# Attention and a state-space scan on one core: weight pieces by DMA, first projections split, one more rotation on VectorE, and a new hand-written order

## The chip, the cores and the metric

The kernel runs on one core of a Trainium2 chip. Its engines take their instructions in order, each from its own queue: TensorE (PE, with weight loads shown apart as PEld), VectorE (DVE), ScalarE (ACT), GpSimd (POOL) and SyncE (SP), which here only issues DMAs. The metric is the device time of one execution in microseconds (us). Before the change it is 131.46 us, the median of three runs (131.37 to 131.47).

## The reference

Two independent parts work on 2048 tokens of width 448, and their results stand side by side in the output (2048 x 896, bfloat16).

```python
# A: attention, 16 heads of 28, each token looks at 8 tokens: itself and 2, 4 ... 14 before it
qkv = x @ wqkv
logits = einsum("bhsd,bhswd->bhsw", q, kg) * 28 ** -0.5     # masked where the index is negative
o = einsum("bhsw,bhswd->bhsd", softmax(logits), vg)
a = o @ wo
# B: a diagonal complex recurrence over time, 448 states
Lam_bar = exp(dt * Lam);  Bu = x @ B_bar.T
h = Lam_bar * h + Bu[t]                                     # for each of 2048 tokens
y = 2 * real(hseq @ Cmat.T) + x * Dskip
out = concatenate([a, y], axis=-1)
```

## The kernel before

Every piece of work is a small function with a short name (marked `@op`), and the string `ORDER` lists some 550 steps. The steps are carried out in that order, so each engine's queue is the string with the other engines' steps left out. In a step such as `QK021@65` the digits behind the name are arguments and those behind `@` the PSUM banks (eight of 2 KB in a partition) that it takes; a dot or an equals sign at the end of a copy out of PSUM says ScalarE or VectorE. A bank is free again only when the step that reads it is done.

**Part A.** x is cut into two halves `u` of 1024 tokens, and each into two blocks `s` of 512. Half 0 is transposed on TensorE (`XI`, `XA`, `XH`, copied into `xT` by `xi`, `xa`, `xh`), half 1 by four DMA transposes (L164), which SP issues behind the loads of half 1 (`xA1`, L148) and of the first part of B's x (`x_load(0)`, L158). The projections contract over 448 = 3 x 128 + 64 rows. `QK(u, m, k)` does group `m` of q or k (0 to 6, even for q and odd for k; 6 holds the last columns of both) for both blocks: with `k` = 0 the three full matmuls of each block, with `k` = 1 the two matmuls over the last 64 rows. Of those, block 0 uses rows 0 to 63 of weights and x, and block 1 rows 64 to 127. So the last 64 weight rows stand twice in `wq[:, 3]`: by DMA in rows 0 to 63 (L135) and copied to rows 64 to 127 by GpSimd (L214, L215). `QS(m, s)` is one block's projection at once, three full matmuls (L347) and the one of 64 rows (L348), for the first two groups of half 0. `wq6` is a tight copy of the last columns, made by GpSimd (L216, L218). `qk` and `qh` copy the results out of PSUM. `V_`/`v` do the same for the values.

`P` multiplies q with four shifted views of k on VectorE (L378; 28 products, of 2048 elements in each partition). `E_` adds them up over the head's 28 channels on TensorE (L390, L394), and `lt`, `TR`, `tr`, `sma`, `smb`, `smc` scale, transpose and normalize. `AL`/`al` line the weights up, `ad` and `sp` send them through DRAM into a banded matrix `PT`, `AV`/`av` multiply it with the values, `W_`/`w`/`ow` multiply with `wo` and store.

**Part B.** The 2048 tokens become 512 groups of T = 4. B's matrix comes transposed by `BD` (one DMA, L651), x by four DMAs `xt` (L675). `BU(g, jp, k)` projects x for state group `g` (7 of them), with k as in `QK`, `BR` adds the rotated previous position, `z` and `y` copy out of PSUM; `UP`, `sa`, `sb`, `sd` scan over the group sums on VectorE, `DN`/`dn` finish them. Then the state before a group is rotated into the group's positions j = 0, 1, 2 for each g, 21 rotations, in one of two ways:

- `H_(j, g)` is one 128 x 512 matmul (L767), and `h(j, g)` adds its result to Z on VectorE (L772);
- `sw(g)` sends a half-swapped copy to `BT` by two DMAs (L790, L791), and `ha`/`hb` (or `ka`/`kb`, the same code) do two VectorE steps (L796, L800).

The order before has twelve of the first kind and nine of the second. At the end 16 blocks `C(j, ct)` are each seven matmuls of 448 columns (L831), `c` adds the skip term on VectorE (L837) and `oc` stores 112 KB from SP (L841). `xd` prepares the skip term. `tf`, `ts`, `rb`, `ca`, `cs` and the `p` steps make tables and coefficients; `tx` and `tz` touch an activation function so that ScalarE loads its table then.

Of the kernel before, what the change touches and what calls it, by code (L numbers as in the profile page):

```python
# [37 lines left out]
qh000. qh011. v000= qh101. QK110@70 P010 E_00@4 qh001. E_02 E_04 xt3 ts13 QK111 P031 QK121@31 qh100. QK141@65 qh111.
QK140 hc0 qk111. ts23 qk141. ts25 QK120 qk140. qk120. QK100@05 qk121. P050 qk110. V_410@63 hc1 qh110. QK101 P061 P011
qk100. qk101. V_411 E_01@1 tf2 ts02 P051 LC P030 E_03 tf6 E_05 QK130@72 P060 E_06 QK151@05 v411. v410. QK131 qk130.  # L40
P101 qk131. P111 lt00 P110 QK150 qk151. V_500@36 V_501 qk150. V_511@72 lt01 P131 v501. V_401@45 TR0@0 V_400 ts06 V_510
E_11@1 tr0. P100 v500. v401. v400. v511. v510. P130 E_13 E_10@6 sma0 smb0 P121 P141 BU401@03 OZ P150 BU201@54 BU301@27
BU300 P120 XR P151 z30. ci1. ci2. BU200 z20. CD1 BR31 ts12 ci3. BU400 z40. P140 z31. ci0. BU000@25 BR21 E_12 z21. E_14
E_15 P160 BU001 BU311@07 z00. CD3 P161 E_16 lt11 lt10 BR41 z41. BU310 BR32 TR1@4 tr1. z32. BU210@21 CD0 smc0 CD2 AL0@6
BR01 BU101@34 sma1 al0. z01. BR33 rb3 BU100 z10= ca6 BU010@06 smb1 xd1 ad0 ts16 BR11 BU211 tx z11. BU111@53 cs6 BU011
BR02 OP smc1 z33. BR22 BU110 z02. BR03 ca3 z03. BR12 BU500@40 UP0 pm3 z12. BR13 z22. BR23 y0. UP3 cs3 AL1@5 z13. z23.
wo UP1 y1. pm0 xd2 AL2@2 pm4 sp0 UP2 y3. BU410@63 y2. al1= BU411 al2. BU501 ts22 BU511@75 z50. BU601@12 BR42 ca4 BU600
ad1 z60. BR51 z51. BU510 sa0 sb0 sd0 DN1@4 BU611@10 cs4 BR52 z42. BR43 AL3@6 ad2 dn1 z52. al3. BR61 z43. sa2 BR53
H_01@4 pm1 sp1 DN0@7 dn0 z53. BU610 z61. BR62 UP5 ts26 UP4 AV001@6 av001. y5. AV020@7 y4. av020. pm2 h01 z62. AV021@2
sb2 ad3 av021. AV031@4 av031. sd2 AV010@6 AV011@5 AV000@3 sp2 AV030@7 av011. DN3@1 W_11@2 H_11@4 av000. av030. av010.  # L50
w11. W_31@5 sa4 sb4 sd4 h11 DN2@3 dn2 ca0 W_00@7 W_10@6 w10. w00. W_01@2 sp3 dn3 DN5@4 w31. dn5 cs0 W_21@6 BR63 H_02@3
ow31 DN4@7 dn4 H_22@1 H_20@5 h22 h20 w01. z63. H_12@4 h12 ow10 ow11 H_10@2 W_30@7 UP6 H_13@1 ha24 W_20@5 h10 ca1 y6.
ca5 AV111@0 av111. AV121@4 AV130@2 ow01 ow00 w30. sa6 av130. AV131@0 AV100@7 h02 av100. sw4 hb24 AV120@2 AV110@3
av131. av110. AV101@7 H_21@0 av120. w20. ow20 sb6 ha14 ow30 av121. w21. W_60@3 ow21 W_70@2 cs1 av101. H_23@5 sd6 sw5
DN6@4 W_50@6 W_40@7 ca2 ha15 dn6 sw6 h13 h23 cs2 W_41@4 w41. hb14 ow41 W_51@1 cs5 C33@5 w50. ha25 w60. ow60 w40. ha16
H_00@4 hb25 W_61@6 ka05 hb15 hb16 W_71@3 C31@7 ow50 w70. w71. ha26 H_03@2 h00 c31 C12@3 h21 C30@4 hb26 xd0 C20@7 ka04
w51. kb05 ow70 C10@1 c10 C32@0 w61. c20 oc31 C13@6 c12 oc12 xd3 c13 c32 ow71 oc13 oc10 ka06 C21@1 C23@7 c30 c21 oc30
C22@3 oc21 c23 oc20 kb04 oc23 oc32 ow51 h03 kb06 c33 C11@6 c22 c11 oc11 C00@0 c00 oc00 C03@4 ow61 oc33 c03 oc03 C01@1
c01 C02@7 oc22 ow40 c02 oc01 oc02
"""  # L60

@with_exitstack
def kernel(
# [276 lines left out]

    @op
    def QS(m, s):

        p = ps()
        pp.setdefault(("qk", 0, m), {})[s] = p
        for kt in range(3):
            PE.matmul(p[:], wqk(m, slice(0, 128), kt), xT[:, 0, 4 * s + kt], start=(kt == 0), stop=False)  # L347
        PE.matmul(p[:], wqk(m, slice(64 * s, 64 * s + 64), 3), xT[64 * s:64 * s + 64, 0, 3], start=False, stop=True)  # L348
# [571 lines left out]
```

## Time and profile before

| what | value |
|---|---|
| median of three runs | 131.46 us |
| the profiled execution, its own time | 131.66 us |
| its span, first to last record | 129.95 us |
| first matmul of a projection (QS00) starts | 6.52 us |
| VectorE's first copy of the second x block (xa10) starts | 9.31 us |
| last 640-byte weight loads land (second L135) | 10.57 us |
| last DMA transpose of half 1 of x lands | 22.27 us |
| first matmul that uses half 1 (QK161) | 23.85 us |
| first scan step (sa0) starts | 71.79 us |
| last matmul ends, last add ends | 126.48, 127.14 us |

The profile's busy time of an engine is the time with at least one instruction running. Matmuls are pipelined, so the time that one costs is the distance from its start to the next one's start. Idle time stands in brackets, with what ended it. A DMA is issued (the time on SP's queue) and lands later, when its data is in place; "landing" is the latter.

### The profile page before, as it was taken

The numbers are of one execution on the slowest core, as the hardware profiler recorded it, in microseconds if no ns is written. First come the engines' busy times: TensorE is split into PE (matmuls) and PEld (weight loads), VectorE is DVE, ScalarE is ACT, GpSimd is POOL, SyncE is SP. The second block draws the span as 40 slices with busy tenths as digits, with TensorE's granted clock in tenths as the row PEclk, the third lists the DMA queues.
The fourth block names the chain that finished last, engine by engine and source line by source line (L and its number), as shares of the span: only waits on it lengthen the run. The fifth ranks groups of instructions, "written<-read, shape, count | busy, mean of one in ns | idle before, by whom it ended". The sixth has DMA issues, their size and how long they took to land.

```text
span 129.9 us, 2872 instructions
## 1 busy us (share of the span) xinstructions
PE 123.9 (95%) x1071; PEld 62.8 (48%) x1071; DVE 119.0 (92%) x211; ACT 90.9 (70%) x185; POOL 23.0 (18%) x45
## 2 busy tenths in 40 slices
PE   6899999999989999999999999999999999999990
PEld 6843445343423434435446335945694554555540
DVE  5679999999999999999999999999999999999941
ACT  3459899999974999987999987999889651000000
...
GB/s 99 196 315 270 308 214 166 229 221 237 167 204 213 226 192 343 240 136 71 203 186 138 273 259 239 209 153 91 184 29 89 110 129 6 34 71 139 144 208 110
DMA packets 44838, 22.91 MB, mean 176 GB/s; under 512 B 31064, under 2 KB 43800, under 8 KB 44824
## 3 DMA queue, kind: packets, MB, share of 16 engines
...
q8 instruction: 8, 0.13, 0.4%
...
HBM read 11.56 MB, written 6.29 MB: 137 GB/s over the span
## 4 chain that ended last, share of the span: by engine, by line
PE 57%; DVE 28%; ACT 9%; issue 3%; DVEq 0%
PE ps L238 21%; DVE pr L378 13%; PE ps L831 13%; PE ps L524 4%; PE ps L701 4%; PE ps L511 3%; DVE Ak L796 3%; PE ps L256 2%; PE ps L347 2%; DVE Z L800 2%; DVE Z L772 2%; ACT kh L114 2%; ACT qf L114 1%; DVE Cw L667 1%; ACT qh_t L114 1%
## 5 line engine op out<-in xcount | busy, mean ns | idle before, releaser
L378 DVE TENSOR_TENSOR pr<-qf,kf 128x2048 bf16<-128x2048 bf16 x24 | 28.4, 1231 | 0.0
L238 PE MATMUL ps<-xbuf,BT 128*128 128x512 bf16 (+1 forms) x112 | 24.0, 379 | 0.0
L831 PE MATMUL ps<-Cw,Z 128*128 128x448 bf16 x112 | 21.8, 352 | 0.1
L238 PE MATMUL ps<-xT,wq 128*128 128x512 bf16 (+1 forms) x96 | 19.7, 380 | 0.0
L114 ACT CAST Z<-ps 128x512 bf16<-128x512 f32 (+1 forms) x34 | 15.7, 503 | 0.9 <-PE ps L713 0.5
L831 PEld LDWEIGHTS <-Z 128*128 128x128 bf16 x112 | 11.0, 98 | 10.5 <-issue 0.3
L238 PEld LDWEIGHTS <-BT 128*128 128x128 bf16 (+1 forms) x112 | 9.1, 97 | 11.7 <-issue 2.4
L524 PE MATMUL ps<-wo,oT 128*128 128x448 bf16 x64 | 13.6, 353 | 0.0
L238 PEld LDWEIGHTS <-wq 128*128 128x128 bf16 (+1 forms) x96 | 7.5, 97 | 11.5 <-issue 4.0
L238 PE MATMUL ps<-wq,xT 128*128 128x448 bf16 (+1 forms) x64 | 12.0, 353 | 0.0
L877 POOL MEMSET PT<- 128x4320 f32 x3 | 11.0, 3699 | 0.0
L837 DVE TENSOR_TENSOR xbuf<-ps,xnB 128x448 bf16<-128x448 f32 x16 | 9.2, 619 | 2.0 <-PE ps L831 1.7
L114 ACT CAST oT<-ps 128x512 bf16<-128x512 f32 x17 | 9.5, 626 | 1.4 <-PE ps L511 1.4
L114 ACT CAST ya<-ps 128x448 bf16<-128x448 f32 (+1 forms) x17 | 8.4, 557 | 2.8 <-issue 1.6
L663 ACT ACTIVATE ctmp<-Cw,c2t 64x448 f32<-64x448 bf16 x14 | 9.3, 666 | 0.3
L114 ACT CAST kf<-ps 128x512 bf16<-128x512 f32 x12 | 6.8, 596 | 3.5 <-PE ps L238 2.5
L524 PEld LDWEIGHTS <-oT 128*128 128x128 bf16 x64 | 6.1, 98 | 5.7 <-ACT oT L114 0.6
L511 PE MATMUL ps<-PT,v_s 128*32 128x135 bf16 (+1 forms) x256 | 8.4, 299 | 0.0
L238 PEld LDWEIGHTS <-xT 128*128 128x128 bf16 (+1 forms) x64 | 5.3, 97 | 5.5 <-issue 1.1
L772 DVE TENSOR_TENSOR Z<-ps,Z 128x512 bf16<-128x512 f32 x12 | 7.9, 682 | 0.0
L114 ACT CAST v_s<-ps 128x448 bf16<-128x448 f32 x15 | 7.3, 541 | 0.5 <-PE ps L238 0.5
L511 PEld LDWEIGHTS <-v_s 128*32 128x32 bf16 x256 | 7.1, 112 | 0.2 <-issue 0.2
...
## 6 DMA issues: line engine op xcount, KB each, us to landing
...
```

What stands on the lines that cost most here:

```text
L114: (ACT.copy if e == "A" else V.tensor_copy)(o, i)
L238: PE.matmul(o, l, r, start=(first and i == 0), stop=(not first and i == len(pairs) - 1 and not more[s]))
L378: V.tensor_tensor(t[:], q.unsqueeze(1).to_broadcast((128, 4, 512)), k4, ALU.mult)
L511: PE.matmul(p[32 * hh:32 * hh + 32, 128 * bl:128 * bl + n], v_s[:, t, 4 * hg + hh, :], PT[:, t % NS, (4 * hg + hh) // HS, (4 * hg + hh) % ...
L524: PE.matmul(p[:, 0:D], late["oT"][:, b // 4, hg, par, 128 * (b % 4):128 * (b % 4) + 128], late["wo"][:, hg, :], start=(hg == 0), stop=(hg ...
L663: ACT.activation(t[a:a + 64, 0:D], Cw[b:b + 64, g, :], ACTF.Copy, scale=c2t[a:a + 64, g:g + 1])
L701: PE.matmul(pp["z", g, j][:], rot(g, 0), late["Z"][:, g, j - 1, :], start=False, stop=True)
L772: V.tensor_tensor(zz, pp.pop(("h", j, g))[:], zz, ALU.add)
L796: e.scalar_tensor_tensor(t.rearrange("p (a n) -> p a n", a=2), prev(g), co2[:, 0, j, g:g + 1], late["Z"][:, g, j, :].rearrange("p (a n) -> ...
L831: PE.matmul(p[:, 0:D], z, Cw[:, g, :], start=(g == 0), stop=(g == G - 1))
L837: V.tensor_tensor(yo, pp.pop(("c", j, ct))[:, 0:D], xnB[:, ct, j, :], ALU.add)
L877: POOL.memset(late["PT"][:, 4 * i:4 * i + 4].rearrange("p t g n -> p (t g n)").bitcast(F32), 0.0)
```

## The change

- `QS` becomes `QA`: only the three full matmuls. The 64-row matmuls of groups 0 and 1 are now steps `QK001` and `QK011`, which add to the open sum in the banks that `QA` took.
- Rows 64 to 127 of `wq[:, 3]` and all of `wq6` come by DMA; GpSimd's five copies go. The first short piece (rows 0 to 63, 128 columns of q and k) is issued from ScalarE's queue, ahead of its three small loads `raw`.
- `H_23`/`h23` become `sw3`, `ha23`, `hb23`, so ten of the 21 rotations are on VectorE.
- The last block of C is (0, 3), in two column halves `CH1`, `CH0`, with their own adds and stores; block (0, 0)'s store and the last half's go out from ScalarE's queue.
- Copies out of PSUM change engine: to ScalarE xi00, xi21, xa11, qk001, v000, z10; to VectorE xi30, xi20, xh1, y0, y1, z50, z51.
- `ORDER` is written anew throughout. Among what moves: `XA10`, `XA11` and `XH1` come right behind the first `QA`; `rb2`, `rb3`, `rb1`, `pg` come ahead of the first product `P000`; `BD` comes ahead of all `xt` on SP; the first use of half 1 is `QK100` instead of `QK161`.

```diff
 ORDER = """
-WU@0 XI0@12 xi30. xi00= XI1@3 xi31. xi01= xi20. xi21= PP@4 pcopy pa pb pe pc QS00@5 pd_ QS10@6 qk010. XA10@7 XH1@1
-qk000. xh1. xt1 XA11@0 pf xt2 xa10= xa11= QS11@3 qk011. QK050@24 QK051 tf0 ts00 P000 QK021@65 QK041@70 QK031@13 tf1
...
+WU@0 XI0@12 xi30= PP@3 pcopy XI1@4 xi00. xi20= pa pb xi01= pe xi21. QA00@5 XA10@6 pd_ xa10= tf0 XA11@7 XH1@1 pc QA10@3
+BD xh1= xa11. tf3 QA01@2 QA11@0 xi31. QK011 QK031@67 QK001 pf pg pk rb2 qk000. QK021@41 qk010. ts00 QK030 qk030. QK020
+ts03 ts13 rb3 qk001. qk031. xt2 V_100@53 V_101 QK041@62 qk020. xt0 v100. qk011. v101. V_111@74 V_110 v110. QK040
+QK050@50 V_011@37 ts10 ts20 v111. rb1 qk040. V_001@46 P000 QK051 V_010 P020 V_000 qk041. ts23 qk050. QK100@25 P021 tf1
...
+oc21 ow70 oc12 oc01 c11 oc30 c00 oc11 oa00 c02 ch1 oc02 oh1 CH0@1 ch0 oh0
 """
...
+    def half_load(q, r, c, n):
+        q.dma_start(qk_s[r:r + 64, 3, :, c:c + n], qk_d[384:448, :, c:c + n])
+
+    half_load(ACT, 0, 0, 128)
     raw = const.tile([G, 3, 2, 64], BF16, tag="raw")
...
     def qk_load(c, n):
         for a in range(2):
             SP.dma_start(qk_s[:, 0:3, a, c:c + n], qk_d[0:384, a, c:c + n].rearrange("(f p) n -> p f n", p=128))
-        SP.dma_start(qk_s[0:64, 3, :, c:c + n], qk_d[384:448, :, c:c + n])
...
-    qk_load(128, 320)
+    qk_load(128, 256)
+    half_load(SP, 0, 128, 256)
+    half_load(SP, 64, 0, 384)
...
+    wq6 = s2.tile([128, 4, 2, 64], BF16, tag="wq6")
+    for a in range(2):
+        SP.dma_start(wq6[:, 0:3, a], qk_d[0:384, a, 384:D].rearrange("(f p) n -> p f n", p=128))
+    for s in range(2):
+        SP.dma_start(wq6[64 * s:64 * s + 64, 3], qk_d[384:448, :, 384:D])
...
-    wq6 = s2.tile([128, 4, 2, 64], BF16, tag="wq6")
-    POOL.tensor_copy(qk_s[64:128, 3, :, 0:128], qk_s[0:64, 3, :, 0:128])
-    POOL.tensor_copy(qk_s[64:128, 3, :, 128:384], qk_s[0:64, 3, :, 128:384])
-    POOL.tensor_copy(wq6[:, 0:3], qk_s[:, 0:3, :, 384:D])
-    for s in range(2):
-        POOL.tensor_copy(wq6[64 * s:64 * s + 64, 3], qk_s[0:64, 3, :, 384:D])
...
     def QK(u, m, k):
-        p = two("qk", u, m)
+        p = pp["qk", u, m] if u == 0 and m < 2 else two("qk", u, m)
...
-    def QS(m, s):
+    def QA(m, s):
 
         p = ps()
         pp.setdefault(("qk", 0, m), {})[s] = p
+        begun.add(("qk", 0, m))
         for kt in range(3):
             PE.matmul(p[:], wqk(m, slice(0, 128), kt), xT[:, 0, 4 * s + kt], start=(kt == 0), stop=False)
-        PE.matmul(p[:], wqk(m, slice(64 * s, 64 * s + 64), 3), xT[64 * s:64 * s + 64, 0, 3], start=False, stop=True)
...
+    @op
+    def oa(j, ct):
+        ACT.dma_start(out_b[j, ct // 2, ct % 2, :, D:2 * D], pp.pop(("yo", j, ct)))
+
+    LAST, CUT = (0, 3), (0, 224, 448)
+
+    @op
+    def CH(i):
+        j, ct = LAST
+        p = pp["ch", i] = ps()
+        n = CUT[i + 1] - CUT[i]
+        for g in range(G):
...
+            PE.matmul(p[:, 0:n], z, Cw[:, g, CUT[i]:CUT[i + 1]], start=(g == 0), stop=(g == G - 1))
+
+    @op
+    def ch(i):
...
+        V.tensor_tensor(yo[:, sl], pp.pop(("ch", i))[:, 0:CUT[i + 1] - CUT[i]], xnB[:, ct, j, sl], ALU.add)
+
+    @op
+    def oh(i):
+        j, ct = LAST
+        (ACT if i == 0 else SP).dma_start(out_b[j, ct // 2, ct % 2, :, D + CUT[i]:D + CUT[i + 1]], pp.pop(("yo", "part", i))[:, CUT[i]:CUT[i + 1]])
```

More of the change, by code (lines that the diff above doesn't have):

```diff
@@ L32 @@
 ORDER = """
-WU@0 XI0@12 xi30. xi00= XI1@3 xi31. xi01= xi20. xi21= PP@4 pcopy pa pb pe pc QS00@5 pd_ QS10@6 qk010. XA10@7 XH1@1
-qk000. xh1. xt1 XA11@0 pf xt2 xa10= xa11= QS11@3 qk011. QK050@24 QK051 tf0 ts00 P000 QK021@65 QK041@70 QK031@13 tf1
-qk051. ts10 ts01 ts20 QK030 QK020 qk031. qk020. pg qk050. qk030. tf4 BD pk QK040 QS01@4 V_001@36 qk041. V_111@21
-qk040. V_011@07 V_010 ts11 ts21 V_110 ts04 v010. v011. rb2 qk021. tz rb0 v110. V_000 P020 V_100@07 ts14 ts24 tf3 V_101
-P021 v001. rb1 v111. P040 QK161@52 QK061@61 v101. tf5 v100. P001 QK060 QK160 ts03 ts05 ts15 qh010. xt0 P041 qk001=
@@ L38 @@
[L38 to L57, printed above, removed]
@@ new lines @@
+QK050@50 V_011@37 ts10 ts20 v111. rb1 qk040. V_001@46 P000 QK051 V_010 P020 V_000 qk041. ts23 qk050. QK100@25 P021 tf1
+qk021. tf5 ts01 rb0 ts11 ts21 ts05 ts15 v011. P001 v010. QK101 qk100. P040 qk101. QK061@17 QK060 qh000. QK110@32
+E_00@5 P041 v001. ts25 E_02 E_04 qk051. qh001. QK111 v000. qh010. P010 tf2 qh011. tf4 P011 qk110. xt3 hc0 QK121@60
+P030 QK161@14 QK160 qh111. QK120 qk120. qh110. QK130@73 P050 E_01@6 P031 qk121. E_03 qh101. qk111. ts02 P051 E_05 ts12
+QK131 qk130. QK151@40 QK150 qk151. V_500@27 V_501 qk150. ts22 qk131. P060 QK141@04 P061 E_06 v501. lt00 P100 P101
@@ new lines @@
+QK140 qk141. P110 xt1 V_410@37 P131 V_401@54 lt01 V_411 v500. ts04 qk140. V_511@62 V_510 P111 v411. v410. TR0@0 v510.
+V_400 P130 tr0. qh100. v401. E_11@7 E_10@3 E_13 v511. BU301@60 tf6 v400. BU401@14 P120 LC sma0 BU201@25 hc1 P160 OZ
+BU300 P150 smb0 z30. P121 XR BU400 z40. BU200 ci1. BR41 z20. BU000@61 BR31 P141 E_12 P140 P151 E_14 E_15 ci2. CD2 CD1
+z31. ci0. ci3. BU001 BU311@20 CD0 P161 E_16 z41. lt10 BU310 lt11 TR1@4 z00. BR32 smc0 tr1. BU210@37 AL0@6 z32. BR01
+al0. BR33 BR21 BU500@42 z21. sma1 smb1 xd1 CD3 OP pm0 BU501 ca6 BU101@65 pm3 BU211 BR22 z50= z22. z01. ad0 wo xd3
@@ new lines @@
+BU100 z10. BU010@43 ca3 BU111@16 BU011 BR02 z02. BR11 z11. cs6 BU110 smc1 ts14 BR12 z12. pm1 z33. BR23 AL1@4 cs3 al1=
+BR03 BR13 BR51 sp0 z51= z23. AL2@5 z13. UP1 y1= UP3 z03. UP2 ad1 UP0 y3. BU410@14 pm4 al2. ad2 BU611@26 BU511@05 y2.
+BU411 y0= sa0 BU601@37 BR42 ts06 ts16 BU510 BR52 z42. BR43 tz ca4 z52. AL3@1 al3. ts24 sb0 BU600 z60. BR53 sp1 z43.
+z53. sd0 DN0@0 BU610 UP4 y4. cs4 DN1@1 UP5 BR61 AV020@3 z61. AV000@4 AV010@7 y5. pm2 av020. AV031@5 av010. av031.
+AV011@3 AV001@7 sa2 sb2 dn0 AV030@0 AV021@5 BR62 av000. av011. ad3 av030. W_30@4 sp2 av001. sd2 sa4 dn1 sb4 DN3@3 dn3
@@ new lines @@
+av021. W_01@0 z62. W_10@7 w30. sp3 H_10@5 w01. ow01 W_31@1 DN2@2 ca1 W_21@4 BR63 sd4 h10 w31. ow30 DN4@0 dn4 H_21@3
+h21 DN5@1 dn5 sw5 dn2 cs1 w10. ha24 z63. ha23 H_11@7 h11 sw4 ca2 W_00@5 w00. ts26 W_11@0 w11. W_20@3 UP6 H_01@1 H_13@2
+h01 H_20@5 h20 y6. sa6 w21. AV130@0 AV110@6 w20. ca0 xd2 AV101@7 AV120@4 av120. AV100@3 sb6 av100. ow11 AV131@1 ow31
+AV121@5 AV111@4 cs2 sd6 ow10 av130. H_22@3 av110. W_70@0 W_40@6 av121. av101. ha25 av111. av131. hb25 w40. W_71@5 ow00
+cs0 W_61@7 W_41@4 h22 DN6@1 sw3 W_60@6 ow40 ca5 ha15 cs5 C32@3 dn6 sw6 hb15 H_12@1 ha26 w60. c32 w70. hb23 hb24 C31@6
@@ L60 @@
+w71. C33@0 c31 H_00@5 ow20 hb26 ha16 ka04 h12 W_51@3 ha14 oc32 C22@6 ow21 w41. w61. c33 C20@4 H_02@7 C21@1 ka05 h13
+C30@0 hb16 xd0 C23@2 hb14 tx w51. C10@3 ow61 c20 C11@4 kb05 h00 c23 h02 ow60 oc20 oc33 ka06 c22 C13@5 c13 c10 H_03@2
+oc23 oc31 ow51 W_50@7 oc13 ow41 ow71 h03 kb04 C12@6 kb06 C01@5 C00@3 c21 c01 oc10 C02@2 w50. ow50 oc22 c12 c30 CH1@7
+oc21 ow70 oc12 oc01 c11 oc30 c00 oc11 oa00 c02 ch1 oc02 oh1 CH0@1 ch0 oh0
 """
@@ L123 @@
     wq_r = A_wqkv[0:384].rearrange("(f p) n -> p f n", p=128)
+    qk_s = wq[:, :, 0:2 * D].rearrange("p k (a n) -> p k a n", a=2)
+    qk_d = A_wqkv[:, 0:2 * D].rearrange("f (a n) -> f a n", a=2)
+    def half_load(q, r, c, n):
+        q.dma_start(qk_s[r:r + 64, 3, :, c:c + n], qk_d[384:448, :, c:c + n])
+    half_load(ACT, 0, 0, 128)
     raw = const.tile([G, 3, 2, 64], BF16, tag="raw")
@@ L841, in oc @@
         SP.dma_start(out_b[j, ct // 2, ct % 2, :, D:2 * D], pp.pop(("yo", j, ct)))
+    @op
[8 more added lines that the diff above has]
+        for g in range(G):
+            z = late["Z"][:, g, j, 128 * ct:128 * ct + 128] if j < T - 1 else \
+                late["Z3"][:, g, (EV, OD)[ct // 2] + 128 * (ct % 2):(EV, OD)[ct // 2] + 128 * (ct % 2) + 128]
+            PE.matmul(p[:, 0:n], z, Cw[:, g, CUT[i]:CUT[i + 1]], start=(g == 0), stop=(g == G - 1))
+    @op
+    def ch(i):
+        j, ct = LAST
+        yo = pp["yo", "part", i] = xnA[:, late["m"] % 8]
+        late["m"] += 1
+        sl = slice(CUT[i], CUT[i + 1])
+        V.tensor_tensor(yo[:, sl], pp.pop(("ch", i))[:, 0:CUT[i + 1] - CUT[i]], xnB[:, ct, j, sl], ALU.add)
+    @op
+    def oh(i):
+        j, ct = LAST
+        (ACT if i == 0 else SP).dma_start(out_b[j, ct // 2, ct % 2, :, D + CUT[i]:D + CUT[i + 1]], pp.pop(("yo", "part", i))[:, CUT[i]:CUT[i + 1]])
     late = {}
```

4 lines of the change are left out of this document (removed).

## The prediction

> **What bounds the kernel now.** I read the page's busy times first, then the shares of the chain of waits, then a table of stages, then TensorE's and VectorE's timelines around the head and the tail.
>
> ```profile
> span 129.9 us, 2872 instructions
> ...
> PE 123.9 (95%) x1071; PEld 62.8 (48%) x1071; DVE 119.0 (92%) x211; ACT 90.9 (70%) x185; POOL 23.0 (18%) x45
> ...
> PE 57%; DVE 28%; ACT 9%; issue 3%; DVEq 0%
> ```
>
> Two engines are nearly full and the chain passes between them. The stages (us; busy PE, PEld, DVE, ACT, POOL; clock; DMA) show where either has room:
>
> ```profile
> 6.50:10.20 3.70, 3.35 (x25) 1.64 (x25) 2.78 (x16) 2.23 (x9) 0.34 (x1) 1.00 1.10 308
> 10.20:57.10 46.90, 46.33 (x332) 18.79 (x331) 45.93 (x71) 42.43 (x86) 3.70 (x9) 1.00 1.08 226
> ...
> 71.80:121.40 49.60, 49.52 (x516) 27.68 (x514) 48.25 (x93) 30.80 (x60) 2.74 (x1) 1.00 0.53 137
> 121.40:129.95 8.55, 5.08 (x27) 2.45 (x25) 4.00 (x7) 0.00 (x0) 0.00 (x0) 1.00 0.45 144
> ```
>
> From 10.2 to 121.4 both PE and DVE have about 1% to spare, so an edit gains only if it shortens both queues, or one of them where the other can follow. DMA is full (1.08 to 1.10) up to 57 us. The head and the tail are where time lies open:
>
> ```profile
> 6.52 0.81 PE L347 MATMUL ps<-xT,wq 128*128 128x512 bf16 x3 [0.42 <-DVE xT L114]
> 7.26 0.39 PE L348 MATMUL ps<-xT,wq 64*128 64x512 bf16 x1
> 7.58 0.82 PE L347 MATMUL ps<-xT,wq 128*128 128x512 bf16 x3
> 8.33 0.39 PE L348 MATMUL ps<-xT,wq 64*128 64x512 bf16 x1
> 8.65 0.62 PE L306 MATMUL ps<-ident,xbuf 128*128 128x128 bf16 x8
> ...
> 10.05 0.81 PE L347 MATMUL ps<-xT,wq 128*128 128x512 bf16 x3 [0.33 <-DVE xT L114]
> ...
> 10.63 0.88 DVE L621 SCALAR_TENSOR_TENSOR fr<-iot,fT,kM 128x256 f32<-128x256 f32 x1
> ...
> 11.43 1.52 DVE L378 TENSOR_TENSOR pr<-qf,kf 128x2048 bf16<-128x2048 bf16 x1
> ...
> 125.19 0.62 DVE L837 TENSOR_TENSOR xbuf<-ps,xnB 128x448 bf16<-128x448 f32 x1 [0.70 <-PE ps L831]
> ...
> 126.52 0.62 DVE L837 TENSOR_TENSOR xbuf<-ps,xnB 128x448 bf16<-128x448 f32 x1 [0.70 <-PE ps L831]
> ```
>
> Starts tell more than durations here, since matmuls overlap: a QS step takes 7.58 - 6.52 = 1.06 us. DVE idles 0.34 + 0.70 + 0.70 = 1.74 us before its last three adds: there PE alone sets the end.
>
> **TensorE's sum.** By starts, a full 512-column matmul takes 0.216 us and a 448-column one 0.189. A 64-row matmul that stands alone in QS makes the matmul ahead of it last 0.312 instead of 0.216 and takes 0.32 itself. Two 64-row ones (a QK, V_ or BU step ending in 1) overlap: QK051, QK021, QK041 and QK031 start at 12.51, 12.74, 12.95 and 13.17, so a pair inside a run costs 0.216.
> - First projections open: four QS at 1.06 (4.24) become four QA at 3 x 0.216 (2.59), and two pairs QK011 and QK001, which join QK031's run, at 0.216 (0.43). Saved 1.22; but QS01's last matmul led into V_001's run already, so 0.1 less: -1.1.
> - Rotations: the old order already has nine on VectorE (six ha, three ka) and twelve on TensorE. Only (2,3) moves: one matmul, -0.22.
> - New order: counting the passages between full, 64-row and 32-column work in both orders, I get 36 and 36, at about 0.1 each: nothing.
> - Last block halved: 7 x 0.189 = 1.32 becomes 14 matmuls of 224 columns, not in the trace. Below, half of 0.189 each, 1.32; above, 0.107 each (128 columns in the warm-up row, 27 in 2.86 us), 1.50. I take 1.35: a weight load in the L831 row lasts 0.098. The add behind the last matmul goes from 0.62 (448) to between 0.31 (half) and 0.42 (the 256-column add, L760): 0.37, -0.25.
>
> The last matmul ended at 126.48: 126.48 - 1.1 - 0.22 + 0.03 = 125.2; plus 0.37 the last add ends at 125.55, against 127.14. PE's own waits (2.7 us in all behind 6.5: 0.5 around XA11, 0.7 before E_01, 0.3 in E_16, the rest small) are kept.
>
> **VectorE's sum.** Taken off: xa11 0.33, qk001 0.60, v000 0.53, z10 0.61, h23 0.60, c03 0.53 = 3.20 (start to start). Put on: xh1 0.33 (as xa11), y0 and y1 0.34 each (as L760), z50 and z51 0.61 each, ha23 and hb23 0.66 each, two half adds 0.34 each = 4.23. Net +1.03. The xi steps before 9 us are swapped about evenly.
> - Earlier start: unbroken work begins with xa10 at 9.31, held by XA10 behind two QS. In the new order XA10 follows one QA and ends at 6.5 + 0.65 + 0.45 = 7.6; DVE gets there through xi01 (till 6.45, as now), pe 1.07 and pd_ 0.43: 7.95. That is -1.3.
> - POOL's five weight copies go (3.2 us, four of them from 10.62 to 13.5). Under them the fr step took 0.88 (0.48 at 13.28) and the first product 1.52 (1.22 at 18.87): -0.7. Their wait for the DMA (3.8 us) held nobody but POOL.
>
> If DVE never waited it would end at 127.14 - 1.74 - 1.3 - 0.7 + 1.03 = 124.4, that is 1.1 us ahead of PE. So PE still sets the end, with little to spare.
>
> **Queues, and what hides what.** SP issues 16 loads up to A's second half instead of 12 (two parts of wq's doubled rows instead of its two short loads, four for wq6): 4 x 0.6 = 2.4 us later, for xA1, x_load(0), the four xT transposes, Bn, x_load(1), and BT's transpose, now ahead of B's. What waits for xA1 is its landing at 15.1, not the issue (9.56), because DMA is full; so the added packet time counts: 1024 of 128 bytes at 13 ns, 128 more of 768 at 39, less 896 x 6 for narrower rows, over 16 engines: 0.8 us. (These are medians of the trace's packet records.) But x_load(0)'s issues, which end at 14.03, end at 16.4 by the 2.4 us, so the transposes start at 16.4 instead of 15.17, and the last lands 1.2 later than 22.27: 23.5. Bounds: +0.8 and +2.4 + 0.8, 23.1 to 25.5. The first user, QK100, now stands earlier. Ahead of it, from QA00 at 6.5, PE has four QA (2.59), the transposes (0.90), four QK (1.295 each) and four V_ (1.135) of full rows, six pairs at 0.216, four at 0.19 and six passages at 0.1: 15.9, so 22.4 (QK161 started at 23.85). PE then waits 1.1 us there. Behind it E_01 and E_16 no longer find their products late (0.7 + 0.3 of the waits kept above), since PE comes to them later and DVE earlier. I take +0.1 on the end.
>
> The Trainium skill, "DMA: Bandwidth & Descriptors", Specifications, says line rate needs 512 bytes or more and that less makes a read-modify-write, which speaks against wq6's 128-byte rows. The trace has such packets at 13 ns against 18 for 256 bytes, so shorter is still cheaper there. Were each charged like 512 bytes (an estimate from the page, 26 ns), the packets would cost 1.7 us instead of 0.8, and the sum would be unchanged, since the issues cost more.
>
> Rows 64 to 127 of wq now come with the ninth SP load, where the second short load stood, which landed at 10.57; QK011 stands at 10.1 by PE's sum: 0.5 of waiting, which makes QK100's shorter by as much. ScalarE's first DMA (0.59) delays `raw` from 2.1 to 2.7; PP moves from 5.87 to 4.8 and was never waited for, cover about 0.5 us. ScalarE has 42.4 of 46.9 us in the middle, and gets one more table load (1.28) at tz, ahead of ca4 and z52, with BR53 behind them: between 0 and 0.4, I take 0. sw3 adds two SP issues (0.6 each) long before hb23. oh0 goes from ScalarE's empty queue.
>
> **Sum.** -1.1 - 0.22 + 0.03 - 0.25 + 0.1 = -1.44, about -1.45. The profiled execution took 131.66 (its span 129.95 and 1.71 around it), so 130.2; the median shown, 131.46, is 0.2 lower: **130.0**.
>
> **Rivals.**
> 1. VectorE's added 1.03 us binds. For it: its 1% of room, and ha23/hb23 in the stretch where the chain runs through DVE (94 to 109). Against: the 1.3 and the 0.7 at the head. If sa0 starts no earlier than 71.79, what follows it grows by 0.87; with the 1.74 used up and 0.5 of waits the last add ends at 127.14 + 0.87 - 1.74 + 0.5 = 126.8: 131.1.
> 2. The second half of A's x lands too late (the other side). One mechanism: four more issues ahead of the transposes, QK100 moved earlier, PE's queue standing behind it. The end moves 1 us for each us past 23.5. It is lost from 24.95 on and measurably slower from 25.2. At the upper bound, 25.5, plus 0.1 for the table load: 132.1. For it: DMA full from 6.5 to 57. Against: the landing follows data more than issues today.
> 3. Waits shrink too: the transposes land by 22.4 after all, and E_01's 0.7 goes without a successor, since DVE has P011 done earlier. Then DVE's 124.4 and PE's 125.55 - 0.7 = 124.85 nearly meet, and the time is 131.46 - 2.29 + 0.1 = 129.3.
> 4. It does less than it says: "ten rotations" is one; that is in the sum.
>
> **How the numbers follow.** Forecast 0.55, rival 1 0.18, rival 2 0.14, rival 3 0.13. A measurement of this kernel tells 0.2%, 0.26 us. Faster: the forecast, rival 3 and about half of rival 1: 0.76; same: 0.08; slower: 0.16. The range takes rival 3 below and most of rival 2: 129.1 to 131.9; the forecast's own is 129.5 to 130.7.
>
> **What would show it.** Right: four first projections at 0.65 us by starts, xa10 at 8.0 to 8.6, POOL empty from 7 to 13 us, the product P000 at 1.22, QK100 waiting about a microsecond at 23 to 24, AL0 1 to 1.6 us before 61.0, last add ending at about 125.7. Wrong: QK100 past 25, E_ steps waiting for products by more than 1 us in sum, sa0 at 71.8 or later, or C's blocks waiting for hb26 or kb06, two SP issues and a landing (2.4 us) behind dn6.

## The result: slower by half a per cent, and the profile after

The changed kernel takes 1.0055 of the time of the kernel before, 95% interval [1.0028, 1.0082], which is 132.2 us against 131.47; 130.0 was forecast. (Ten of its fifteen runs ran at a lower granted clock and are left out of this ratio.) The profiled execution took 132.44 us where that of before took 131.66. So it lost 0.7 us where 1.45 were to be won, and it lost them as rival 2 had it: the second half of A's x lands too late.

First the page of the changed kernel: its span, the busy time of its engines, and the engines' shares of the chain of waits.

```profile
span 130.7 us, 2883 instructions
...
PE 121.5 (93%) x1067; PEld 62.9 (48%) x1077; DVE 119.6 (92%) x214; ACT 93.0 (71%) x185; POOL 19.9 (15%) x40
...
PE 52%; DVE 24%; SPq 13%; DMA 5%; issue 3%; DVEq 0%
```

Before, the chain held PE 57%, DVE 28% and ACT 9%. Now SP's queue has 13% and the DMAs 5%: loads have come onto the path. TensorE has 2.4 us less busy time in a longer span, so it waits. (Ten of its matmuls are missing from this trace, 1067 for 1077 weight loads, so its busy sums are a little low.) Which stage holds them, the table of stages says (from:to, us, busy PE, PEld, DVE, ACT, POOL, clock, DMA, GB/s):

```profile
6.50:10.20 3.70, 2.96 (x25) 1.73 (x27) 3.08 (x15) 2.15 (x9) 0.00 (x0) 1.00 1.10 295
10.20:57.10 46.90, 44.24 (x312) 18.14 (x315) 43.84 (x67) 41.50 (x83) 0.99 (x5) 1.00 0.99 221
...
71.80:121.40 49.60, 49.16 (x529) 28.61 (x530) 48.70 (x95) 33.64 (x68) 1.47 (x1) 1.00 0.52 132
121.40:130.70 9.30, 5.75 (x37) 3.32 (x35) 5.85 (x12) 0.00 (x0) 0.00 (x0) 1.00 0.55 177
```

From 10.2 to 57.1 PE falls from 46.33 to 44.24 us busy and DVE from 45.93 to 43.84, 2.1 us each, in part A and at full clock; the timelines below tell what of it is waiting. The rows of 71.8 to 121.4 hardly differ. Next SP's queue up to the transposes (start, duration, line, what is loaded, how many):

```profile
3.82 0.37 SPq L143 DMA_DIRECT2D xbuf<-in_A_x_dram  x1
4.23 1.04 SPq L138 DMA_DIRECT2D wq<-in_A_wqkv_dram  x2
5.32 1.39 SPq L129 DMA_DIRECT2D wq<-in_A_wqkv_dram  x2
6.75 0.59 SPq L147 DMA_DIRECT2D wq<-in_A_wqkv_dram  x1
7.39 1.13 SPq L149 DMA_DIRECT2D wq<-in_A_wqkv_dram  x2
8.56 1.12 SPq L152 DMA_DIRECT2D wq<-in_A_wqkv_dram  x2
9.73 1.29 SPq L154 DMA_DIRECT2D wq<-in_A_wqkv_dram  x2
11.06 3.02 SPq L158 DMA_DIRECT2D xbuf<-in_A_x_dram  x3
14.13 3.06 SPq L168 DMA_DIRECT2D xnB<-in_B_x_dram  x6
17.31 5.52 SPq L174 DMA_TRANSPOSE xT<-xbuf  x4
```

The same stretch of the kernel before:

```profile
3.69 0.58 SPq L140 DMA_DIRECT2D xbuf<-in_A_x_dram  x1
...
7.88 1.69 SPq L148 DMA_DIRECT2D xbuf<-in_A_x_dram  x3
10.21 3.82 SPq L158 DMA_DIRECT2D xnB<-in_B_x_dram  x6
15.17 5.37 SPq L164 DMA_TRANSPOSE xT<-xbuf  x4
```

Read the rows by their ends. Before, SP finished `x_load(0)` at 14.03 and then stood for 1.1 us until `xA1` had landed: the data set the start of the transposes. After, `xA1` (L158) is issued 3.18 us later, `x_load(0)` ends at 17.19 and the first transpose follows at 17.31 with no gap: now the row of issues sets it, but only just: by the semaphore records of the trace `xA1`'s last load is complete at 17.09 (15.09 before), 0.1 us ahead of the row's end. So the longer row and the later data hold the transposes to almost the same time. The chain of waits of the changed kernel goes on from there (start, us, what):

```profile
17.31 1.35 SPq L174
18.70 1.44 SPq L174
20.19 1.30 SPq L174
21.53 4.12 DMA xT<-xbuf
25.70 4.27 PE ps L242 x20
```

The fourth transpose is issued at 21.53 (19.24 before) and lands 4.12 us later, at 25.65 (3.03 later, at 22.27, before). TensorE's timeline (the bracket is the idle time, and what ended it):

```profile
21.02 2.44 PE L242 MATMUL ps<-wq,xT 128*128 128x448 bf16 x12
25.70 4.70 PE L242 MATMUL ps<-xT,wq 128*128 128x512 bf16 x21 [2.24 <-DMA xT<-xbuf]
```

QK100 stands 2.24 us for half 1: TensorE was ready for it at 23.46. Behind it stand the others. ScalarE's timeline:

```profile
27.52 1.07 ACT L114 CAST qf<-ps 128x512 bf16<-128x512 f32 x2 [2.24 <-PE ps L242]
...
29.83 0.51 ACT L644 ACTIVATE tab<-fr,cols 128x256 bf16<-128x256 f32 x1
```

and VectorE's:

```profile
30.38 0.48 DVE L625 SCALAR_TENSOR_TENSOR fr<-iot,fT,kM 128x256 f32<-128x256 f32 x1 [0.95 <-ACT tab L644]
...
48.29 0.29 DVE L423 TENSOR_TENSOR attn<-attn,mk 128x256 bf16<-128x256 bf16 x1 [0.74 <-ACT attn L114]
```

ScalarE waits the same 2.24 us for QK100's sum. The table step ts25 (L644) is queued behind that copy and ends late; tf4 (L625) then waits 0.95 us for it, since `fr` has two buffers and ts25 still reads the one tf4 is to write. `sma0` (L423) waits another 0.74 us at 48.3 for `tr0`, whose matmuls (`TR0`) stand behind the late blocks on TensorE: from 25.70 the chain of waits runs along TensorE almost without a break up to them, at 46.69. So sa0 starts at 73.68, 1.9 us later than before, and kb06 ends at 122.73, 1.3 us later. Only the tail gives something back. VectorE's last two adds in the changed kernel:

```profile
126.51 0.39 DVE L871 TENSOR_TENSOR xbuf<-ps,xnB 128x224 bf16<-128x224 f32 x1
127.18 0.39 DVE L871 TENSOR_TENSOR xbuf<-ps,xnB 128x224 bf16<-128x224 f32 x1 [0.28 <-PE ps L863]
```

From kb06's end to the last add's end it takes 4.84 us (127.57 - 122.73) where it took 5.74 (127.14 - 121.40): of 1.74 us of waiting 0.28 are left. (It holds one block more: eight are added behind kb06 now, the last in two halves, and seven before.) That 0.9 us is the one gain that arrives.

### The profile page after: what moved, and what is told of

It is laid out like the page before. It is cut to its first block, busy times and chain, and to the rows that moved or that the text cites. A ratio compares the mean times of both kernels' runs of the same rounds, so it can differ in the third digit from the quotient of the medians.

```text
span 130.7 us, 2883 instructions
## 1 busy us (share of the span) xinstructions
PE 121.5 (93%) x1067; PEld 62.9 (48%) x1077; DVE 119.6 (92%) x214; ACT 93.0 (71%) x185; POOL 19.9 (15%) x40
## 3 DMA queue, kind: packets, MB, share of 16 engines
HBM read 11.68 MB, written 6.29 MB: 138 GB/s over the span
## 4 chain that ended last, share of the span: by engine, by line
PE 52%; DVE 24%; SPq 13%; DMA 5%; issue 3%; DVEq 0%
PE ps L242 26%; PE ps L835 15%; PE ps L394 4%; DVE hs L746 3%; DMA xT<-xbuf 3%; SPq L174 3%; DVE p L732 2%; DVE p L731 2%; DVE Z L776 2%; DMA wq<-in_A_wqkv_dram 2%; DVE Cw L671 2%; SPq L158 2%; SPq L168 2%; DVE Ak L800 2%; PE ps L705 2%
## 5 line engine op out<-in xcount | busy, mean ns | idle before, releaser
L382 DVE TENSOR_TENSOR pr<-qf,kf 128x2048 bf16<-128x2048 bf16 x24 | 27.7, 1217 | 0.0
L242 PE MATMUL ps<-xbuf,BT 128*128 128x512 bf16 (+1 forms) x108 | 22.9, 379 | 0.6 <-issue 0.5
L835 PE MATMUL ps<-Cw,Z 128*128 128x448 bf16 x105 | 20.9, 352 | 0.2
L114 ACT CAST Z<-ps 128x512 bf16<-128x512 f32 (+1 forms) x31 | 14.6, 508 | 1.2 <-PE ps L705 0.6
L835 PEld LDWEIGHTS <-Z 128*128 128x128 bf16 x105 | 10.2, 98 | 10.3 <-issue 0.7
L114 ACT CAST qf<-ps 128x512 bf16<-128x512 f32 x12 | 6.8, 588 | 3.3 <-PE ps L242 3.2
L114 ACT CAST oT<-ps 128x512 bf16<-128x512 f32 x17 | 8.8, 605 | 0.4 <-PE ps L515 0.4
L841 DVE TENSOR_TENSOR xbuf<-ps,xnB 128x448 bf16<-128x448 f32 x15 | 8.6, 613 | 0.0
L114 ACT CAST v_s<-ps 128x448 bf16<-128x448 f32 x16 | 8.0, 542 | 0.1
L776 DVE TENSOR_TENSOR Z<-ps,Z 128x512 bf16<-128x512 f32 x11 | 7.3, 679 | 0.0
```

Of the source, the lines that this page charges most:

```text
L114: (ACT.copy if e == "A" else V.tensor_copy)(o, i)
L382: V.tensor_tensor(t[:], q.unsqueeze(1).to_broadcast((128, 4, 512)), k4, ALU.mult)
L776: V.tensor_tensor(zz, pp.pop(("h", j, g))[:], zz, ALU.add)
L835: PE.matmul(p[:, 0:D], z, Cw[:, g, :], start=(g == 0), stop=(g == G - 1))
L841: V.tensor_tensor(yo, pp.pop(("c", j, ct))[:, 0:D], xnB[:, ct, j, :], ALU.add)
```

## The experiments

Each kernel was timed in five rounds beside the kernel before (its median 131.47 to 131.7 in these sets). A ratio below is to the kernel before; times "in the profile" are of one execution. Two theories stood: the late half of x (rival 2), and VectorE's added work (rival 1).

**e1_wq6_pool**: `wq6` made by GpSimd's copies again, its four DMAs off SP.

```diff
-    qk_load(128, 256)
-    half_load(SP, 0, 128, 256)
+    qk_load(128, 320)
+    half_load(SP, 0, 128, 320)
     half_load(SP, 64, 0, 384)
...
-    for a in range(2):
-        SP.dma_start(wq6[:, 0:3, a], qk_d[0:384, a, 384:D].rearrange("(f p) n -> p f n", p=128))
-    for s in range(2):
-        SP.dma_start(wq6[64 * s:64 * s + 64, 3], qk_d[384:448, :, 384:D])
...
+    POOL.tensor_copy(wq6[:, 0:3], qk_s[:, 0:3, :, 384:D])
+    for s in range(2):
+        POOL.tensor_copy(wq6[64 * s:64 * s + 64, 3], qk_s[0:64, 3, :, 384:D])
```

> The changed kernel, but GpSimd makes wq6 by its three copies again, so SP issues four loads fewer ahead of the second half of A's x. Late theory (the changed kernel is slow because the last transpose of half 1 lands at 25.65 us and QK100 waits for it): the transposes start at about 15 us instead of 17.31, the last lands at 22.8 to 23.5, QK100 starts there, and the time falls by 1.5 to 2.2 us against the changed kernel, to 130.0 to 130.7, below the kernel before (131.47). Rival, VectorE's added 1.03 us binds: QK100 starts earlier, but the end hardly moves, 131.5 to 132.2. Rival, the number of bytes and not of issues sets the landing (DMA is full in that stage): the last transpose still lands at 25 or later and the time stays at 132.

Measured: 0.9926 [0.9901, 0.9951]. TensorE's line at QK100:

```profile
23.65 3.61 PE L241 MATMUL ps<-xT,wq 128*128 128x512 bf16 x17 [0.42 <-DMA xT<-xbuf]
```

The wait is 0.42 instead of 2.24, VectorE's waits of 0.95 and 0.74 behind it are gone, the last add ends at 125.70, and the kernel is now 0.7% faster than before. (SP now waits 1.6 us for `xA1`'s data, so the transposes start at 16.45 and not, as expected, at about 15.) So the four DMAs cost the change 1.3% (1.0055 against 0.9926), 1.7 us, and this holds for rival 2.

**e2_half1_first**: all DMAs kept, but the loads of half 1 stand ahead of `wq6`'s, and `x_load(0)` behind the transposes.

```diff
+    xA1 = xbuf[:, 8 * D:].rearrange("p (t n) -> p t n", n=2 * D)
+    for d0, d1, b, c in ((0, D, 8, 0), (D, 512, 12, 384), (512, 896, 12, 0)):
+        SP.dma_start(xA1[:, :, d0:d1], xA_r[:, b:b + 4, c:c + d1 - d0])
     wq6 = s2.tile([128, 4, 2, 64], BF16, tag="wq6")
...
-    x_load(0)
...
+    x_load(0)
```

> The changed kernel with all its DMAs, only in another order on SP: xA1 ahead of wq6's four loads, and x_load(0) behind the four transposes. Late theory: the transposes are issued as soon as xA1 has landed, at about 15 us, the last lands at 22.5 to 23.5, and the time is 129.8 to 130.6. If the bytes set the landing, no change: 25 and 132. If VectorE binds: 131.5 or more though QK100 starts early. What could spoil it: x_load(0), Bn and BT's transpose come about 1 to 2 us later than in the changed kernel, and the first BU has about 1 us to spare.

Measured: 0.9989 [0.9967, 1.0011]; the transposes are issued from 15.31, QK100 starts at 23.21 with no wait. 0.7% is won back, but not all: 131.34 us, where 129.8 to 130.6 was expected if only the late half costs. What was pushed back is late in its turn: BT's transpose is issued at 32.30 (30.81 in the changed kernel), the last `xt` at 43.47 (41.99), and one `BU` waits 0.40 us. That these make up the rest is argued, not shown.

**e3_weights_as_before**: all weight loads and GpSimd's five copies as before, the rest of the change kept.

```diff
-    half_load(ACT, 0, 0, 128)
...
+    half_load(SP, 0, 0, 128)
...
-    qk_load(128, 256)
-    half_load(SP, 0, 128, 256)
-    half_load(SP, 64, 0, 384)
+    qk_load(128, 320)
+    half_load(SP, 0, 128, 320)
...
+    POOL.tensor_copy(qk_s[64:128, 3, :, 0:128], qk_s[0:64, 3, :, 0:128])
+    POOL.tensor_copy(qk_s[64:128, 3, :, 128:384], qk_s[0:64, 3, :, 128:384])
```

(and `wq6` as in e1_wq6_pool)

> The changed kernel with the weights loaded and copied wholly as before: five GpSimd copies, no load from ScalarE's queue ahead of raw. Late theory: SP is as far as in the kernel before, the last transpose lands at 22.3 to 22.8 and QK100 starts at 22.5 to 23; the rest of the change then shows its worth: 129.8 to 130.5, with GpSimd's copies costing VectorE up to 0.7 us under tf and pg. Rival, the new order or VectorE's added work is what costs: 131.5 to 132.2 even so.

Measured: 0.9906 [0.9888, 0.9924]. Its queue and its QK100:

```profile
15.06 5.59 SPq L168 DMA_TRANSPOSE xT<-xbuf  x4
```

```profile
23.47 3.83 PE L242 MATMUL ps<-xT,wq 128*128 128x512 bf16 x18
```

With the transposes back at 15.06, QK100 starts at 23.47 without a wait. Everything in the change except the weights' loads is worth 0.9%; the loads turn that into a loss of 0.55%, so they cost 1.5% (1.0055 against 0.9906).

**e4_dma_weights_alone**: the other way round, the kernel before with its own order and only the new weight loads.

```diff
...
+    half_load(ACT, 0, 0, 128)
...
-        SP.dma_start(qk_s[0:64, 3, :, c:c + n], qk_d[384:448, :, c:c + n])
...
-    qk_load(128, 320)
+    qk_load(128, 256)
+    half_load(SP, 0, 128, 256)
+    half_load(SP, 64, 0, 384)
...
+    for a in range(2):
+        SP.dma_start(wq6[:, 0:3, a], qk_d[0:384, a, 384:D].rearrange("(f p) n -> p f n", p=128))
+    for s in range(2):
+        SP.dma_start(wq6[64 * s:64 * s + 64, 3], qk_d[384:448, :, 384:D])
...
-    POOL.tensor_copy(qk_s[64:128, 3, :, 0:128], qk_s[0:64, 3, :, 0:128])
```

(and GpSimd's four other copies out)

> The kernel before with only the weights' loads changed (doubled rows and wq6 by DMA, first piece from ScalarE's queue), in the old order. Late theory: half 1 lands at about 25.6 as in the changed kernel, QK161 (23.85 before) waits for it, about 1.8 us, and since ScalarE and VectorE stand behind it the time is 1 to 1.8 us above the kernel before, 132.5 to 133.2. Rival, the loads are harmless and the order costs: 131.4 to 131.7.

Measured: 1.0069 [1.0045, 1.0093], 132.53 us, the low end of what was expected. TensorE at its first use of half 1:

```profile
25.11 3.09 PE L242 MATMUL ps<-xT,wq 64*128 64x512 bf16 x15 [1.57 <-DMA xT<-xbuf]
```

The loads alone are slower, by the same kind of wait in the old order. Here the data and not the row sets the start of the transposes: SP waits 0.9 us for `xA1`, which lands at 17.46. TensorE's wait is shorter, 1.57 us, and the loads cost 0.69% here against 1.5% in the new order. So they do harm by themselves in either order, and more of it in the new one; why more of the wait reaches the end there was not tested.

**g1_wq6_pool_queue**: the changed kernel, the same four `wq6` DMAs, the same bytes and packets, issued from GpSimd's queue.

```diff
-        SP.dma_start(wq6[:, 0:3, a], qk_d[0:384, a, 384:D].rearrange("(f p) n -> p f n", p=128))
+        POOL.dma_start(wq6[:, 0:3, a], qk_d[0:384, a, 384:D].rearrange("(f p) n -> p f n", p=128))
...
-        SP.dma_start(wq6[64 * s:64 * s + 64, 3], qk_d[384:448, :, 384:D])
+        POOL.dma_start(wq6[64 * s:64 * s + 64, 3], qk_d[384:448, :, 384:D])
```

> The changed kernel with the same four DMAs of wq6, same packets and bytes, but issued from GpSimd's queue instead of SP's. If the time that SP spends on the four issues (and the places they take in its row) makes half 1 late: the transposes are issued at 14.8 to 16.5, QK100 starts by 23.7 instead of 25.69, and the time is 130.2 to 130.8. If the number of packets and bytes in the full DMA stage makes it late: QK100 at 25 or later, 131.8 to 132.3. GpSimd's issues could themselves disturb VectorE's steps at 7 to 12 us, by up to 0.7.

Measured: 0.9965 [0.994, 0.999]. GpSimd's timeline and TensorE's:

```profile
6.34 1.66 POOL L220 DMA_DIRECT2D wq<-in_A_wqkv_dram  x2
8.00 1.20 POOL L222 DMA_DIRECT2D wq<-in_A_wqkv_dram  x2
```

```profile
23.25 2.96 PE L242 MATMUL ps<-xT,wq 128*128 128x512 bf16 x14
```

The four DMAs are still there, QK100 waits for nothing, and `xA1`'s last load is complete at 15.72 instead of 17.09. It was their place in SP's row that made half 1 late, not their bytes or packets. The time, 130.89 us, lies just above the 130.2 to 130.8 expected and 0.5 us above e1's 130.36; what takes this rest is open.

**f1_whole_last**: e1 with the last block whole.

```diff
-oc23 oc31 ow51 W_50@7 oc13 ow41 ow71 h03 kb04 C12@6 kb06 C01@5 C00@3 c21 c01 oc10 C02@2 w50. ow50 oc22 c12 c30 CH1@7
-oc21 ow70 oc12 oc01 c11 oc30 c00 oc11 oa00 c02 ch1 oc02 oh1 CH0@1 ch0 oh0
+oc23 oc31 ow51 W_50@7 oc13 ow41 ow71 h03 kb04 C12@6 kb06 C01@5 C00@3 c21 c01 oc10 C02@2 w50. ow50 oc22 c12 c30 C03@7
+oc21 ow70 oc12 oc01 c11 oc30 c00 oc11 oa00 c02 oc02 c03 oc03
```

> The kernel with wq6 from GpSimd (130.36 us), but its last block of C whole: one group of seven 448-column matmuls, one add, one store from SP. If the halving is worth what the prediction's sum says (-0.25 + 0.03), 130.6. If the shorter add is given back by the second store, 130.3 to 130.4.

Measured: 0.9939 [0.9917, 0.9961], 0.17 us above e1, with intervals that overlap. The last add waits 0.69 us and not 0.28. The sign is as forecast (0.22), the size is not resolved.

**f2_rotation_back** and **g5_rotation_back2**: e1 with the one moved rotation, (2, 3), on TensorE again. In f2 its add h23 stands ahead of DN6, in g5 right behind its matmul.

```diff
-h21 DN5@1 dn5 sw5 dn2 cs1 w10. ha24 z63. ha23 H_11@7 h11 sw4 ca2 W_00@5 w00. ts26 W_11@0 w11. W_20@3 UP6 H_01@1 H_13@2
+h21 DN5@1 dn5 sw5 dn2 cs1 w10. ha24 z63. H_11@7 h11 sw4 ca2 W_00@5 w00. ts26 W_11@0 w11. W_20@3 UP6 H_01@1 H_13@2
...
-AV121@5 AV111@4 cs2 sd6 ow10 av130. H_22@3 av110. W_70@0 W_40@6 av121. av101. ha25 av111. av131. hb25 w40. W_71@5 ow00
-cs0 W_61@7 W_41@4 h22 DN6@1 sw3 W_60@6 ow40 ca5 ha15 cs5 C32@3 dn6 sw6 hb15 H_12@1 ha26 w60. c32 w70. hb23 hb24 C31@6
+AV121@5 AV111@4 cs2 sd6 ow10 av130. H_22@3 av110. W_70@0 W_40@6 av121. av101. ha25 av111. av131. hb25 w40. W_71@5 H_23@1 ow00
+cs0 W_61@7 W_41@4 h22 h23 DN6@1 W_60@6 ow40 ca5 ha15 cs5 C32@3 dn6 sw6 hb15 H_12@1 ha26 w60. c32 w70. hb24 C31@6
```

> The kernel with wq6 from GpSimd (130.36 us), but the rotation (2,3) on TensorE again: one matmul more (0.22 us), and on VectorE one add (0.60) in place of two steps (1.32). If VectorE's queue sets the time behind sa0, 129.6 to 129.9. If TensorE does, 130.5 to 130.6. If each waits for the other about equally, 130.3 to 130.4.

> As the kernel with the rotation (2,3) on TensorE again (130.81 us), with its add placed right behind the matmul, since DN6 waits for the add's bank and C32 then started 0.8 late. If that wait was what cost: 130.2 to 130.4, the rotation's place is worth nothing. If TensorE's 0.22 reaches the end: 130.5 to 130.6. If it stays at 130.8, more than the matmul is lost.

Measured: f2 0.9954 [0.9936, 0.9971], 0.3% above e1; g5 0.9919 [0.9897, 0.9942], which can't be told from e1's 0.9926. f2's 130.81 us lies in none of its three ranges. TensorE's line in f2 shows a wait that none of them had:

```profile
101.22 0.27 PE L731 MATMUL ps<-Z,R 128*128 128x256 bf16 x1 [0.59 <-DVE Z L749]
```

DN6 takes bank 1, and waited 0.59 us until h23 had read it. That was the place chosen for h23, not the rotation. With h23 earlier the rotation's move is worth nothing that can be measured; g5's interval, 0.3 us to either side, is wider than the 0.22 in question.

**f3_first_closed**: e3 with the first projections closed, as `QS`, the 64-row steps QK001 and QK011 dropped and xi31 moved ahead of QS00, which needs it. (The function `QA`, with its fourth matmul back, is left out here.)

```diff
-WU@0 XI0@12 xi30= PP@3 pcopy XI1@4 xi00. xi20= pa pb xi01= pe xi21. QA00@5 XA10@6 pd_ xa10= tf0 XA11@7 XH1@1 pc QA10@3
-BD xh1= xa11. tf3 QA01@2 QA11@0 xi31. QK011 QK031@67 QK001 pf pg pk rb2 qk000. QK021@41 qk010. ts00 QK030 qk030. QK020
+WU@0 XI0@12 xi30= PP@3 pcopy XI1@4 xi00. xi20= pa pb xi01= pe xi21. xi31. QS00@5 XA10@6 pd_ xa10= tf0 XA11@7 XH1@1 pc QS10@3
+BD xh1= xa11. tf3 QS01@2 QS11@0 QK031@67 pf pg pk rb2 qk000. QK021@41 qk010. ts00 QK030 qk030. QK020
```

> The kernel with the weights loaded as before (130.40 us), but the first projections closed again: four QS, no QK001 and QK011, xi31 ahead of the first. If the 1.1 us of TensorE time that opening them saves reaches the end, 131.4 to 131.6. If VectorE's product stage covers the head, QK100 starts about 1 us later but the time rises by only 0 to 0.5, to 130.4 to 130.9.

Measured: 0.9896 [0.9876, 0.9917], below what either theory allowed and not to be told from e3's 0.9906. QK100 starts at 23.82, 0.35 us later than in e3, and the end does not come later. Opening the projections, the largest term of the forecast, is worth nothing that can be measured here; its 1.1 us would be 0.8%. The next runs ask what holds the head instead.

**f4_pb_later** (e3), **g3_x_first** (f3) and **g4_open_x_first** (e3): VectorE's small step `pb` moved behind xi01, so that the first projection starts earlier. In g3 and g4 the load of x blocks 4 to 7 also goes ahead of the first short weight piece (in g3 the first line has f3's QS for QA).

```diff
-WU@0 XI0@12 xi30= PP@3 pcopy XI1@4 xi00. xi20= pa pb xi01= pe xi21. QA00@5 XA10@6 pd_ xa10= tf0 XA11@7 XH1@1 pc QA10@3
+WU@0 XI0@12 xi30= PP@3 pcopy XI1@4 xi00. xi20= pa xi01= pb pe xi21. QA00@5 XA10@6 pd_ xa10= tf0 XA11@7 XH1@1 pc QA10@3
...
-    half_load(SP, 0, 0, 128)
     SP.dma_start(xnA[:, 4:8], xA_r[:, 4:8])
+    half_load(SP, 0, 0, 128)
```

> The kernel with the weights loaded as before (130.40 us), with one step moved: pb (two small VectorE steps that wait for ScalarE's pa) behind xi01. xi01 ended at 6.8 us instead of the 6.45 of the prediction, since pb stands ahead of it; QA00 then starts 0.3 to 0.4 earlier than 6.87. If the head is on the path, 130.0 to 130.1; if it is covered, 130.4. A version that may beat all so far.

> The kernel with closed first projections (129.97 us), with the load of x's blocks 4 to 7 one place earlier on SP (ahead of the short weight piece) and pb behind xi01. XA10 waited for that load until 7.93 and VectorE's unbroken row (xa10, 8.59) stands behind it. If this head sets the time: xa10 at 7.9 to 8.1, the last add 0.4 to 0.7 earlier, 129.3 to 129.6. If products or a later landing take over: 129.9 to 130.1. A version that may beat all.

> The kernel with the weights loaded as before (open first projections, 130.40 us), with pb behind xi01 and the load of x's blocks 4 to 7 one place earlier, ahead of the short weight piece, which an open QA00 does not need. Theory: opening the projections was worth nothing because XA10 had to wait for that load (7.93 to 8.2) whatever stood ahead of it; now QA00 starts at about 6.05 and ends at 6.7, XA10 starts at 7.2 to 7.5, xa10 at 7.9 to 8.1 instead of 8.82, and the last add ends 0.5 to 0.9 earlier: 129.4 to 129.8. If the head is not on the path after all: 130.2 to 130.4.

Measured: f4 0.9914 [0.989, 0.9937], g3 0.9934 [0.9911, 0.9956], g4 0.9896 [0.9874, 0.9918]. By their medians (130.24, 130.61 and 130.35 us) none falls into the range in which the head sets the time. In f4 QA00 starts 0.6 us earlier (6.29 instead of 6.87), but XA10 not (8.30 against 8.16), since it waits for x blocks 4 to 7. That wait stands in e3's TensorE timeline too:

```profile
8.16 0.84 PE L310 MATMUL ps<-ident,xbuf 128*128 128x128 bf16 x12 [0.48 <-DMA xbuf<-in_A_x_dram]
```

In g3 the short piece is what came late. Its QS00 needs it for the 64-row matmul, which waited 1.38 us:

```profile
8.27 0.39 PE L326 MATMUL ps<-xT,wq 64*128 64x512 bf16 x1 [1.38 <-DMA wq<-in_A_wqkv_dram]
```

Only g4, open and with x first, moves the head: XA10 at 7.53, xa10 at 8.19 instead of e3's 8.82, sa0 at 71.70 instead of 72.24, the last add at 125.61 instead of 126.17. In the profile what the head wins goes through to the end (it shows the fastest of g4's five executions, 129.88 us); in the ratios g4, f3 and e3 can't be told apart. g4 and f3 have the best, 0.9896: 1.0% faster than before and 1.6% faster than the changed kernel.

## Why the prediction was wrong

**The step that failed is "Queues, and what hides what"**: "the transposes start at 16.4 instead of 15.17, and the last lands 1.2 later than 22.27: 23.5", and "I take +0.1 on the end". The mechanism was seen (issues that take the place of a landing), its size and its cover were not. Both ways to the transposes were priced too low: the row of issues at 2.4 us later (measured 3.16, from 14.03 to 17.19) and `xA1`'s landing at 0.8 (measured 2.0). (The 1.7 us of packets that it estimates at 26 ns each comes to 1.64 by its own numbers.) Measured are 17.31 and 25.65, past the upper bound of 25.5 too, and 1.7 to 2.0 us on the end (e1 and e3 against the changed kernel, 1.0055 - 0.9926 and 1.0055 - 0.9906) in place of 0.1. Of the 3.38 us by which the last transpose lands later, 2.29 is the later issue and 1.09 the longer landing behind it. Two of the signs named for being wrong came: QK100 past 25, and sa0 later than 71.8. The parts:

- Five issues more, not four, stand between the loads of x blocks 4 to 7 and `xA1`: a second half row and four of `wq6`; from L143's issue to `xA1`'s first it takes 3.05 us longer. One short load ahead of the x blocks went to ScalarE, which the sum of four credits. But its time was not won: L143 still starts at 3.82 (3.69 before). The chain has a DMA in that place:

```profile
0.81 3.00 DMA wq<-in_A_wqkv_dram
3.82 0.37 SPq L143
```

  SP stood 1.0 us (2.84 to 3.82) until a weight piece issued at 0.81 had landed. That is ScalarE's, since SP's first weight load is issued at 1.82, and the trace names the link: L143 waits for semaphore 100, which ScalarE's piece completes at 3.81. 0.13 + 3.05 = 3.18 us, the whole delay of `xA1`.
- The landing takes 4.12 us behind the issue and not 3.03. It is 3.42 in e4 and 2.96 to 3.10 in the traces of the twelve other kernels, so it is long only where `wq6`'s loads stand ahead of `xA1` in SP's row. Why isn't settled.
- Too little cover: 1.1 us of waiting was foreseen, from 22.4 on, and set against the waits of E_01 and E_16 behind it. TensorE was ready only at 23.46, so a landing at 23.5 would have cost nothing; the landing came 2.15 us later than that. TensorE's wait for products is gone, as foreseen (0.5 us before). But the measured 2.24 holds up ScalarE just as long, and through ts25 and tr0 VectorE for 0.95 and 0.74 us. VectorE has no time to make that up: in part A its products stand one behind another.

Rival 2 itself had the price nearly right: lost from a landing at 24.95 on, 1 us for 1 us, so at 25.65 it gives 131.46 + 0.70 = 132.2, and 132.2 was measured. It was the chance of it, 0.14, that was too low, because the bounds of the landing had been added up but the middle had been taken near the low end. That the price fits so well is partly luck. It takes the rest of the change to be worth 1.45 us, and e3 has 1.2 for it, but without the largest term, the opening, and with a gain at the tail in its place.

**First projections open, -1.1: wrong.** The matmuls are saved (TensorE's 64-row steps went into runs), but that row doesn't set the pace. XA10 waits for x blocks 4 to 7 (landing at 7.95, which the prediction left out), and f3 without the opening is as fast. That VectorE's row sets the pace from xa10 on is read from the profile, not tested.

**VectorE's earlier start, -1.3: half.** xa10 starts at 8.65, not at 7.95: 0.66 won. `pb` stands ahead of xi01 in the new order, so QA00 starts at 6.95 and not at 6.5, and XA10 waits 0.24 us for x. TensorE also waited 0.29 us for `raw` at 5.30, for which the prediction had counted a cover of 0.5. g4 shows that what is moved here moves everything behind it.

**GpSimd's copies, -0.7 on VectorE:** not measured by itself. The copies are gone in the changed kernel (POOL 0.99 us from 10.2 to 57.1, 3.70 before), but the late half hides any gain. With the copies back, in e3, tf3's two steps lasted 0.53 and 0.66 us, against 0.35 and 0.48 in the changed kernel: 0.36 us. The first product takes 1.22 us in both, since the new order has it at 17.3 to 17.6, behind the copies.

**The last block halved, -0.25 + 0.03:** the add takes 0.39 (0.37 forecast). On the end f1 puts it at 0.17 us, within the interval. **The rotation, -0.22:** not resolved (g5).

**Rival 1, VectorE's 1.03 us:** in part it holds. In e3, where half 1 is in time, sa0 starts at 72.24 (71.79 before) and kb06 ends at 121.33 (121.40): up to there nothing is gained, with one block's add fewer done by kb06. In e1 it is 0.54 us by then (71.76 and 120.86). e3's 0.97 us (127.14 - 126.17) is the tail, where from kb06 to the last add 4.84 us are needed instead of 5.74. At most some 0.2 of these come from the halving (f1) and nothing that can be measured from the rotation (g5); that the rest is the new order of the last blocks is an inference by elimination, since no run tried the order alone.
